# Memory attention with a sticky expert layer: the token sums of the first softmax as one product a group instead of one a head

## The chip, the cores and the metric

The kernel runs on one core of a Trainium2 chip. The time is that of the device for one launch, in microseconds (us); lower is better. The core has a matrix engine (PE; its weight loads are listed apart as PEld), a vector engine (DVE), a scalar engine (ACT), a general engine (POOL) and a queue that issues transfers (SP). They run side by side and wait for one another through semaphores.

## What is computed

For each of 8 batches and 8 heads, 576 tokens with 64 features each are squeezed into 32 memory rows, which are then attended to. The output of that goes through an expert layer whose expert "sticks" from token to token. The part that matters here is the first softmax, over the tokens (axis 2):

```python
def _attn_ref(q, k, v, phi):
    a = phi - np.max(phi, axis=2, keepdims=True)
    a = np.exp(a)
    a = a / (np.sum(a, axis=2, keepdims=True) + 1e-09)
    k_m = np.einsum('bhsm,bhsd->bhmd', a, k)
    v_m = np.einsum('bhsm,bhsd->bhmd', a, v)
    ...
    attn = softmax(scale * q @ k_m.T)          # over the 32 memory rows
    return attn @ v_m
def _moe_ref(x, w_gate, w_local, w1, w2):
    ...
    out[b, s] = p[e] * (np.maximum(x[b, s] @ w1[e], 0.0) @ w2[e])
```

The divisor `np.sum(a, axis=2)` is one number for each batch, head and memory row: 8 heads by 32 rows, 256 numbers a batch.

## The kernel before

The heads of a batch stand in two groups (`NG` = 2) of four (`HG` = 4). Head 2h + g has its 576 tokens on the 64 partitions `half[g]`: partitions 0 to 63 for group 0, 64 to 127 for group 1, nine tokens on each. A tile of 128 partitions so holds both groups at once.

For each batch the chain of the first softmax runs through these steps, each a function and a name in the list of steps:

- "phi", "kv": the transfers of phi and of k and v. "colmax" to "cx": a maximum over all tokens. "sub", "exp": subtraction and exponential, in place in `pt`.
- "asum" (L310, on DVE; in batch 0 L386 and L387, in batch 1 on POOL): adds the nine tokens of a partition, so that `asum` is 128 partitions by 4 heads by 32 memory rows.
- "pkv" (L396): the unnormalised `k_m` and `v_m`. 72 products a batch, each with weights of 64 partitions by 32 columns (one head, one of nine tokens) and 128 moving columns; the output goes to 32 partitions of the accumulator `pkv[g]`, those of head h.
- "sums" (`f_sums`, L407): adds `asum` over the 64 partitions of a group, by a product with a column of ones. Eight products a batch, each with weights of 64 partitions by 32 columns and one moving column; the output is column 128 of `pkv[g]`, partitions 32h to 32h + 31.
- "rinv" (L418, L419, on DVE): adds 1e-9 to that column and takes the reciprocal. "kvn" (L427, on ACT; one in batch 0 on DVE, L429): scales `pkv` by it. "pT" (L435), "kvT" (L440): transpose and copy. `kvT` is what the scores (`k_psc`, L507), the first expert product (`w_pg`, L787) and the gate (`f_pgg`, L453) read.

The rest of the time of PE goes to the expert layer: the hidden part "ph" (L819) and the output part "po" (L857 to L859 and, for the turned half, L907 to L909), with 128 weight columns and 256 to 512 moving columns each.

The order on every engine is written out by hand. The steps of batch 0, and the first ones of batch 1, stand in `start()`, with `warm(n)` issuing n idle products "wp" (L305) between them. After that the loop over the batches runs through the expert layer of batch b, and a table of places (`PLACES`) says how far into it each step of the later batches is put in. For "sums" the table gives one number a batch. In batches 1 to 4 the products of the sums stand between two products of the expert layer; in batch 0 and in batches 5 to 7 they come right behind those of "pkv". Neither the table nor any other order is altered.

## Time and profile before

| what | value |
|---|---|
| median of 3 runs | 415.64 us (414.85 to 418.31) |
| the profiled execution's own time | 416.56 us |
| span of its instructions | 414.8 us |
| granted TensorE clock, mean over the span | 0.999 |
| records of L407 (sums) in the trace, PE and PEld each | 128, from 14.8 to 303.5 us |

In this page each product with 32-bit weights is listed as two records, a weight load (PEld) and a matmul (PE) for each of two passes: the 8 batches with 8 products of the sums each make 64 products and 128 records. A line with "x16" is a run of 16 such records, with the start of the first and the time from there to the end of the last. "64*32" is the form in which a product takes the array: 64 rows and 32 columns.

The span is the time from the first instruction to the last; the execution's own time is 1.8 us longer.

### The profile page before, as it was taken

What the parts mean: (1) busy time and instruction counts of PE and PEld (TensorE: products, weight loads), DVE (VectorE), ACT (ScalarE), POOL (GpSimd) and SP (SyncE); (2) the same over time, 40 slices, a digit from 0 to 9 for tenths busy, and PEclk for the clock granted to TensorE, in tenths of its full rate; (3) what the DMA queues carried; (4) which work ended last, traced back from release to release, by engine and by line L of the source; (5) the groups of instructions that cost most, each with busy time, mean ns of one, the idle gap of its engine ahead of it and who ended that gap; (6) DMA issues with size and microseconds to landing.
All of it is one profiled execution on the core that took longest, in us unless ns stands there. A gap on an engine that the chain in (4) does not pass through costs nothing.

```text
span 414.8 us, 10606 instructions
## 1 busy us (share of the span) xinstructions
PE 395.0 (95%) x4195; PEld 326.7 (79%) x4195; DVE 284.4 (69%) x714; ACT 177.8 (43%) x427; POOL 150.9 (36%) x162
## 2 busy tenths in 40 slices
PE   8778898999999989999999999999999999999994
PEld 2546866798777977699778997789878996899884
DVE  4487788878976797886759767777757676625300
ACT  2154652436442744435541564336541564146010
POOL 3024541536241744038510681029410660156000
PEclk9999999999999999999999999999999999999999
DMA  8969793999197939798789198965974087202011
GB/s 238 286 224 291 167 372 122 199 283 378 31 351 127 371 131 246 174 379 299 228 162 399 37 300 152 297 244 164 241 134 170 2 246 253 82 0 65 25 40 55
DMA packets 115445, 82.58 MB, mean 199 GB/s; under 512 B 69616, under 2 KB 89088, under 8 KB 115392
## 3 DMA queue, kind: packets, MB, share of 16 engines
q1 hardware_dynamic: 115328, 81.84, 66.4%
q8 instruction: 35, 0.57, 0.6%
q14 instruction: 18, 0.15, 0.1%
q0 software_dynamic: 64, 0.02, 0.1%
HBM read 66.60 MB, written 15.24 MB: 197 GB/s over the span
## 4 chain that ended last, share of the span: by engine, by line
PE 79%; DMA 11%; DVE 5%; issue 1%; SPq 1%; ACT 1%; DVEq 0%
PE ph L819 22%; PE po L907 8%; PE po L857 8%; PE po L908 7%; PE po L909 7%; PE po L859 7%; PE po L858 7%; DMA att_d<-at 6%; DMA kv_t<-in_v_dram 5%; PE pkv L396 4%; PE pg L787 3%; PE psc L507 2%; PE pl L604 1%; DVE h L829 1%; PE po L881 1%
## 5 line engine op out<-in xcount | busy, mean ns | idle before, releaser
L777 POOL TENSOR_TENSOR w2l<-raw,w2h 128x512 fp32r<-128x512 f32 x64 | 82.0, 1303 | 31.2 <-ACT w2h L776 23.5
L819 PE MATMUL ph<-ah,Gh 128*128 128x256 f32 (+1 forms) x256 | 74.5, 306 | 1.4 <-DVE h L829 1.3
L829 DVE SCALAR_TENSOR_TENSOR h<-ph,h 128x320 fp32r<-128x320 f32 (+2 forms) x104 | 52.7, 519 | 31.9 <-ACT h L827 31.5
L819 PE MATMUL ph<-ah,Gl 128*128 128x256 f32 (+1 forms) x256 | 71.6, 295 | 0.0
L907 PE MATMUL po<-h,w2l 128*128 128x320 f32 x224 | 71.5, 319 | 0.0
L909 PE MATMUL po<-h,w2h 128*128 128x320 f32 x224 | 69.2, 309 | 0.0
L908 PE MATMUL po<-h,w2h 128*128 128x320 f32 x224 | 69.2, 309 | 0.0
L827 ACT ACTIVATE h<-ph 128x320 fp32r<-128x320 f32 (+1 forms) x96 | 46.4, 489 | 44.7 <-PE ph L819 44.4
L857 PE MATMUL po<-w2h,h 128*128 128x512 f32 (+1 forms) x152 | 60.7, 399 | 0.0
L914 POOL TENSOR_TENSOR oT<-oT,gT 128x320 f32<-128x320 f32 x28 | 20.7, 741 | 104.3 <-DVE oT L913 97.4
L859 PE MATMUL po<-w2h,h 128*128 128x512 f32 (+1 forms) x152 | 57.8, 380 | 0.0
L858 PE MATMUL po<-w2l,h 128*128 128x512 f32 (+1 forms) x152 | 57.7, 379 | 0.0
L819 PE MATMUL ph<-al,Gh 128*128 128x256 f32 (+1 forms) x256 | 54.8, 295 | 0.0
L819 PEld LDWEIGHTS ph<-ah,Gh 128*128 128x128 f32 x256 | 48.1, 188 | 7.6 <-issue 3.6
L819 PEld LDWEIGHTS ph<-ah,Gl 128*128 128x128 f32 x256 | 48.2, 188 | 0.0
L563 POOL TENSOR_TENSOR al<-at,ah 128x576 fp32r<-128x576 f32 (+1 forms) x18 | 23.1, 1289 | 64.7 <-ACT ah L559 42.8
L907 PEld LDWEIGHTS po<-h,w2l 128*128 128x128 f32 x224 | 42.0, 188 | 5.6 <-issue 5.2
L776 ACT ACTIVATE w2h<-raw 128x512 fp32r<-128x512 f32 x64 | 38.4, 625 | 11.9 <-PE po L909 10.1
L908 PEld LDWEIGHTS po<-h,w2h 128*128 128x128 f32 x224 | 42.1, 188 | 0.2
L909 PEld LDWEIGHTS po<-h,w2h 128*128 128x128 f32 x224 | 42.1, 188 | 0.0
L819 PEld LDWEIGHTS ph<-al,Gh 128*128 128x128 f32 x256 | 41.1, 188 | 0.1
L857 PEld LDWEIGHTS po<-w2h,h 128*128 128x128 f32 x152 | 28.6, 188 | 14.3 <-issue 9.4
(153 smaller groups left out, 578.6 us busy)
## 6 DMA issues: line engine op xcount, KB each, us to landing
raw<-in_moe_w_dram SPq DMA_DIRECT2D x34, 512.0 KB, 6.2
raw<-in_moe_w_dram SPq DMA_DIRECT2D x15, 1024.0 KB, 6.9
kv_t<-in_k_dram SPq DMA_DIRECT2D x7, 1152.0 KB, 8.7
kv_t<-in_v_dram SPq DMA_DIRECT2D x7, 1152.0 KB, 11.2
q_t<-in_q_dram SPq DMA_DIRECT2D x112, 72.0 KB, 3.3
att_d<-at SPq DMA_DIRECT2D x8, 576.0 KB, 9.8
out_dram<-oT SPq DMA_DIRECT2D x28, 160.0 KB, 5.6
out_dram<-ot SPq DMA_DIRECT2D x17, 256.0 KB, 6.0
```

What stands on the lines that cost most here:

```text
L563: (eng or nc.gpsimd).tensor_tensor(out=st.al[:, gs, ss], in0=st.at[:, gs, ss], in1=st.ah[:, gs, ss], op=ALU.subtract)
L776: nc.scalar.activation(h, src, AF.Copy)
L777: nc.gpsimd.tensor_tensor(out=l, in0=src, in1=h, op=ALU.subtract)
L819: nc.tensor.matmul(pv[:, c - c0], lhsT=lt[:, g, cs], rhs=rt[:, g, s0 : s0 + n], start=(i == 0), stop=(i == 5),)
L827: nc.scalar.activation(hc[:, :, 0:n], pv, AF.Relu)
L829: nc.vector.scalar_tensor_tensor(out=hc[:, :, o : o + z - a], in0=pv[:, :, a:z], scalar=0.0, in1=hc[:, :, a:z], op0=ALU.max, op1=ALU.subtract,
L857: nc.tensor.matmul(po[:, c0:c1], lhsT=h[:, c, th], rhs=hi, start=(c == 0), stop=False)
L858: nc.tensor.matmul(po[:, c0:c1], lhsT=h[:, c, th], rhs=lo, start=False, stop=False)
L859: nc.tensor.matmul(po[:, c0:c1], lhsT=h[:, c, tl], rhs=hi, start=False, stop=(c == FC - 1))
L907: nc.tensor.matmul(po[:, 0:n], lhsT=lo, rhs=h[:, c, 0:n], start=(c == 0), stop=False)
L908: nc.tensor.matmul(po[:, 0:n], lhsT=hi, rhs=h[:, c, 0:n], start=False, stop=False)
L909: nc.tensor.matmul(po[:, 0:n], lhsT=hi, rhs=h[:, c, n : 2 * n], start=False, stop=(c == FC - 1))
```

## The change

`f_sums` issues one product for each group instead of one for each group and head. Its weights are the four heads' sums side by side, 64 partitions by 128 columns, and its output is the whole column 128 of `pkv[g]`, all 128 partitions. The same numbers come out at the same places: row 32h + m of the output is the sum of head h and memory row m. The number of products falls from 64 to 16 in the whole kernel.

```diff
     def f_sums(st):
-        for h in range(HG):
-            for g in range(NG):
-                nc.tensor.matmul(
-                    st.pkv[g][32 * h : 32 * h + 32, P : P + 1],
-                    lhsT=st.asum[half[g], h],
-                    rhs=ones[half[g]],
-                    start=True,
-                    stop=True,
-                )
+        for g in range(NG):
+            nc.tensor.matmul(
+                st.pkv[g][:, P : P + 1],
+                lhsT=st.asum[half[g]].rearrange("p h m -> p (h m)"),
+                rhs=ones[half[g]],
+                start=True,
+                stop=True,
+            )
```

Each engine keeps its order. Behind the edit every line number is smaller by one, so that L407 becomes L406 and L435 becomes L434.

On PE in batch 5, where the sums stand right behind "pkv" (an output of 32 partitions by 128 columns reads 32x128), before:

```order
L396 MATMUL pkv<-kv_t,phi_t 32x128 [waits Activation_49]
L396 MATMUL pkv<-kv_t,phi_t 32x128 x23
L407 MATMUL pkv<-ones,asum 32x1 [waits DVE_49]
L407 MATMUL pkv<-ones,asum 32x1 x7
L857 MATMUL po<-w2h,h_2872 128x512
```

and after:

```order
L396 MATMUL pkv<-kv_t,phi_t 32x128 [waits Activation_49]
L396 MATMUL pkv<-kv_t,phi_t 32x128 x23
L406 MATMUL pkv<-ones,asum 128x1 [waits DVE_49]
L406 MATMUL pkv<-ones,asum 128x1
L856 MATMUL po<-w2h,h_2842 128x512
```

The two products stand where the eight stood, the first of them with the same wait for DVE, and the next neighbours are the same.

On PE in batch 4, where the sums stand between products of the expert layer, there is one more difference, some rows further on, at the transposes pT. Before:

```order
L859 MATMUL po<-w2h,h_2150 128x512
L407 MATMUL pkv<-ones,asum 32x1 [waits DVE_49]
L407 MATMUL pkv<-ones,asum 32x1 x7
L857 MATMUL po<-w2h,h_2150 128x512
...
L435 MATMUL pT<-ident,kvn 128x128 [waits Activation_49] x2
```

and after:

```order
L858 MATMUL po<-w2h,h_2126 128x512
L406 MATMUL pkv<-ones,asum 128x1 [waits DVE_49]
L406 MATMUL pkv<-ones,asum 128x1
L856 MATMUL po<-w2h,h_2126 128x512
...
L434 MATMUL pT<-ident,kvn 128x128 [waits PE_49,Activation_49]
L434 MATMUL pT<-ident,kvn 128x128 [waits Activation_49]
```

The first transpose of batch 4 now also waits for an earlier product of PE itself, the last one of the gate step L604, which stands ahead of the sums. No other wait is added or taken away on any engine.

## The prediction

> **What bounds the kernel now.** I read the page's chain of work first, since it says which engine's time counts.

> ```profile
> PE 395.0 (95%) x4195; PEld 326.7 (79%) x4195; DVE 284.4 (69%) x714; ACT 177.8 (43%) x427; POOL 150.9 (36%) x162
> PE 79%; DMA 11%; DVE 5%; issue 1%; SPq 1%; ACT 1%; DVEq 0%
> ```

> PE is busy for 95% of the span and carries 79% of the chain. A tenth of a microsecond more or less in its queue mostly reaches the end. So the question is what the sums cost PE now, and what they will cost.

> Second, the sums by their own line, with minimum, median and maximum duration.

> ```profile
> L407 PEld LDWEIGHTS pkv<-ones,asum x128: 102/106/107, 14.8 to 303.5; 64*32 64x32 f32 x128
> L407 PE MATMUL pkv<-ones,asum x128: 163/167/188, 14.9 to 303.5; 64*32 64x1 f32 x128
>   DVE rinv L418: 6.2, 3
> ```

> 128 records of some 167 ns would be 21 us one after another. They are not one after another, as the order in time shows. First batch 2, where the sums stand alone between products of form 128*128 (columns: start, duration of the run, engine):

> ```profile
> 86.17 0.31 PE L908 MATMUL po<-h,w2h 128*128 128x320 f32 x1
> 86.32 0.31 PE L909 MATMUL po<-h,w2h 128*128 128x320 f32 x1
> 86.56 0.27 PE L407 MATMUL pkv<-ones,asum 64*32 64x1 f32 x16
> 86.75 0.41 PE L907 MATMUL po<-h,w2l 128*128 128x320 f32 x1
> 87.00 0.30 PE L908 MATMUL po<-h,w2h 128*128 128x320 f32 x1
> ```

> All 16 records take 0.27 us, of which 0.167 is one record: 16 starts lie within 0.10 us. The expert products normally start 0.15 apart (86.17, 86.32). Around the sums two things are added. At each change of form the next product starts only about 0.07 before the end of the last one (86.32 + 0.31 = 86.63 against 86.56; 86.83 against 86.75), so the overlap of neighbours is lost twice. And the first product after it takes 0.41 instead of 0.31.

> Then batch 5, where the sums follow pkv in the same form 64*32, and the place of batch 2 where a product of another form follows pkv directly:

> ```profile
> 209.08 0.63 PE L396 MATMUL pkv<-kv_t,phi_t 64*32 64x128 f32 x27
> 209.45 0.29 PE L407 MATMUL pkv<-ones,asum 64*32 64x1 f32 x16
> 209.68 0.50 PE L857 MATMUL po<-w2h,h 128*128 128x512 f32 x1
> ...
> 84.94 0.61 PE L396 MATMUL pkv<-kv_t,phi_t 64*32 64x128 f32 x26
> 85.48 0.41 PE L907 MATMUL po<-h,w2l 128*128 128x320 f32 x1
> ```

> In the same form the sums start 0.26 before pkv's end (209.71 against 209.45), and they end at 209.74, only 0.03 later than pkv. Into another form the start is 0.07 before the end (85.55 against 85.48). So in batches 0, 5, 6 and 7, where the sums follow pkv, they cost almost nothing now.

> The chain of work over time has the sums in it at every batch; the first, one standing alone, and the last:

> ```profile
> 15.07 0.12 PE pkv L407 x14
> 86.63 0.20 PE pkv L407 x13
> 303.57 0.13 PE pkv L407 x15
> ```

> With four such stretches of about 0.20 and four of about 0.13, plus 0.10 for the first product behind each lone block, 4 x 0.30 + 4 x 0.13 = 1.7 us is all that any change to this step can win.

> **The change part by part.** It removes 12 of the 16 matmul records of each step, and makes the others 128 columns wide instead of 32. What does a wide one cost? No row shows 64 rows by 128 columns with one moving column, so I bound it. Weight loads by width:

> ```profile
> L578 PEld LDWEIGHTS pl<-ggt,at 128*1 128x1 f32 x32 | 1.1, 81 | 4.0 <-issue 1.9 <-DVE at L555 1.3 <-ACT qT L497 0.4
> L355 PEld LDWEIGHTS pm<-ident,mc 128*64 128x64 f32 x32 | 1.6, 134 | 2.3 <-DVE mc L350 0.6 <-issue 0.6 <-DVE l L592 0.4
> L907 PEld LDWEIGHTS po<-h,w2l 128*128 128x128 f32 x224 | 42.0, 188 | 5.6 <-issue 5.2
> ```

> 1, 32, 64 and 128 columns take 81, 105 (the sums now), 134 and 188 ns: some 80 fixed and about 0.84 ns a column, so 107 ns for 128 columns against 25 for 32. The nearest blocks of four records, each behind a change of form:

> ```profile
> 64.13 0.24 PE L578 MATMUL pl<-ggt,at 128*1 128x8 f32 x4 [1.11 <-DVE at L555]
> 22.45 0.44 PE L355 MATMUL pm<-ident,mc 128*64 128x128 f32 x4
> 24.56 0.43 PE L493 MATMUL pq<-ident,q0e 32*128 32x32 f32 x4
> L355 PE MATMUL pm<-ident,mc x32: 272/298/323, 6.8 to 287.2; 128*64 128x128 f32 x32
> L493 PE MATMUL pq<-ident,q0e x8: 221/222/243, 15.1 to 24.8; 32*128 32x32 f32 x8
> ```

> L355 is nearest in kind: two products on two separate parts of the array, two passes each. Its block of 0.44 less one record of 0.27 leaves 0.16 of starts for two passes, so the two products run side by side, and the first pass is longer by 0.05 (323 against 272), which is its load of 64 columns. For the new sums I take the same with 128 columns: the first pass 0.10 longer (as 0.41 against 0.31 at L907), the second 0.107 behind it, the other group 0.007 beside. Starts spread over 0.22 us, and with one record of 0.167 the block takes **0.39 us**. Low end: L493, 128 columns of weights but 32 rows: 0.43 less 0.222 is 0.21 for three steps, the first longer by 0.02, so two passes side by side need 0.02 + 0.063 + 0.007 = 0.09, a block of 0.26. High end: nothing side by side, 0.10 + 3 x 0.107 + 0.167 = 0.59.

> Sums standing alone (batches 1 to 4): 0.39 instead of 0.27, **+0.12 each**; both changes of form are there already. In batch 1 I cost it at nothing:

> ```profile
> 40.34 0.60 ACT L827 ACTIVATE h<-ph 128x512 fp32r<-128x512 f32 x1 [1.86 <-PE ph L819]
> 40.65 0.28 PE L819 MATMUL ph<-ah,Gl 128*128 128x256 f32 x1
> 41.02 0.39 PE L819 MATMUL ph<-ah,Gh 128*128 128x256 f32 x1
> ```

> There PE stands for 0.37 between starts that are otherwise 0.12 apart, until ACT is done at 40.94 with a tile from before the sums: 0.25 of cover for 0.12. Without this cover it would be 0.12 more. So 3 x 0.12 = 0.36.

> Sums behind pkv (batches 0, 5, 6, 7): the form now changes, 64*32 to 64*128, which the trace never shows. If it is a change like the others, the sums start 0.07 before pkv's end instead of 0.26, 0.19 later, and end 0.39 after that: 209.64 + 0.39 = 210.03 against 209.74, **+0.28 each** with the decimals kept, 1.13 in all. If the array keeps going between two forms of 64 rows, it is only the +0.12, or less. I take the change of form as drained, because every change in the rows above is, in both directions. [...] No run so far shows this pair of forms.

> Behind PE: `rinv` on DVE waits for the sums three times (6.2 us in the rows above, most of it idle time in batch 0) and will start 0.1 to 0.3 later. Queued behind it on DVE are transposes and expert evictions; ACT's `kvn` and then pT wait for it. In batch 0 all of it moves with PE, whose queue between sums and pT is filled by idle products, so nothing is added beyond the +0.28. Later pT comes microseconds after the sums. The new wait of pT in batch 4 is for a product that is some microseconds old; the price of such a wait in PE's queue is a 51 ns event, hidden behind products in flight, and 0.05 if not:

> ```profile
> L435 PEldq EVENT_SEMAPHORE  x2: 51/51/51, 16.2 to 309.0; - x2
> ```

> No transfer, SP instruction or POOL instruction is moved.

> Sum: 0.36 + 1.13 = **+1.5 us**, nearly all of it on the chain. The profiled execution took 416.56, with a span of 414.8; it would become 418.1. The median shown is 415.64, 0.9 below that execution, so I forecast **417.1 us**. A change within 1%, 4.2 us, can't be told from none by measuring this kernel; this is 0.4%.

> **The rivals.**

> *Nothing side by side.* The two groups share the 128 columns, and the four passes run one behind another: a block of 0.59, 0.20 more for seven steps, and batch 1 leaves its cover by 0.07. 1.5 + 1.5 = +3.0, 418.6 us. Against it: the eight products of L407 on eight places start 16 records in 0.10, and half of these share their columns with another.

> *The load is cheap.* Block 0.26 as at L493: the lone ones gain nothing, those behind pkv cost 0.19 - 0.03 = 0.16: +0.6, 416.2 us. For it: L493 is the only row with fewer than 128 rows and 128 columns. Against: its weights are for a transpose, and 107 ns fits all the other widths.

> *Cost goes by the number of products.* Four records at the spacing of L578, (0.24 - 0.17) / 3 = 0.025, and no drain between two forms of 64 rows: a block of 0.24, -0.03 for the three lone ones and -0.04 for the four others (0.26 early and 0.24 long, it ends before pkv, and the next starts 0.07 before pkv's end, at 209.64 instead of 209.68), -0.25 us: 415.4. Against it: the width of the load would have to cost nothing. [...]

> *A transfer slips.* The side of a clear loss. The chain has this stretch, and the page's list of transfers the median of its kind:

> ```profile
> 50.16 12.93 DMA att_d<-at
> att_d<-at SPq DMA_DIRECT2D x8, 576.0 KB, 9.8
> ```

> This store has 3.1 us above the median when others share the queues. If the delay of 0.28 in batch 0 moves another store of the eight from the median to this, off PE's cover, that is 1.5 + 3.1 = +4.6, 420.2 us. It decides from 2.7 us of slip on. Against it: SP's order stays, and all that leads to these issues moves together.

> **How the numbers follow.** Forecast 55%, cheap load 17%, nothing side by side 14%, by number of products 8%, a transfer slips 5%; 1% for a transfer that happens to come earlier by as much. The first four lie between 415.4 and 418.6. Widened by what the lowest run lies under its median (0.8) below and by half of that above, the range is 414.6 to 419.0. Faster by over 1%: 0.01. Slower by over 1%: the slipped transfer, 0.05. Within 1%: 0.94.

> **What would show it.** In the new profile L406 should have 32 records of form 64*128 with weight loads of about 188 ns, in blocks of four that take 0.39 us (0.26: cheap load; 0.59: nothing side by side; 0.24: by number). In batches 5 to 7 the block should start 0.07 before pkv's end and 0.26 before it if nothing drains. `po` behind it should still have its first record 0.1 longer. Wrong would be the forecast if the span grows or shrinks by more than these blocks do, which would put the cause in another queue.

## The result

The changed kernel took 421.94 us (median of 4 runs, 421.29 to 423.66), against 416.98 us for the one before (median of 4 runs, 414.85 to 418.31). The ratio is 1.0127 with a 95% interval of 1.0089 to 1.0164: slower by 5 us. The interval is clear of no change, and the time lies above the range of 414.6 to 419.0. Its profiled execution took 421.71 us.

The page after, in the lines that answer to those shown of before (PEclk is the clock granted to PE in 40 equal slices of the span, in tenths of full speed):

```profile
span 419.9 us, 10411 instructions
PE 398.3 (95%) x4095; PEld 328.5 (78%) x4099; DVE 285.9 (68%) x714; ACT 177.6 (42%) x427; POOL 151.2 (36%) x162
PE 83%; DMA 7%; DVE 5%; issue 2%; SPq 1%; ACT 1%; DVEq 0%
PEclk9999999999999998999999999999999999999999
```

The span is 5.1 us longer. PE has 96 to 100 records fewer and is busy for 3.3 us more. Two things in it were not forecast: "issue", time in which an engine waits for nothing that the profile shows, is 2% of the chain instead of 1%, and in the sixteenth slice the clock granted to PE is not full.

First the sums themselves. In order of time on PE, batch 2, where they stand alone, and batch 5, where they follow pkv (columns: start, duration of the run, engine):

```profile
85.97 0.31 PE L908 MATMUL po<-h,w2h 128*128 128x320 f32 x1
86.21 0.39 PE L406 MATMUL pkv<-ones,asum 64*128 64x1 f32 x4
86.53 0.42 PE L906 MATMUL po<-h,w2l 128*128 128x320 f32 x1
...
213.23 0.76 PE L396 MATMUL pkv<-kv_t,phi_t 64*32 64x128 f32 x36
213.92 0.39 PE L406 MATMUL pkv<-ones,asum 64*128 64x1 f32 x4
214.23 0.50 PE L856 MATMUL po<-w2h,h 128*128 128x512 f32 x1
```

The block takes 0.39 us in both. In batch 5 it starts at 213.92, 0.07 before pkv ends at 213.99; before the change it was 0.26. So between these two forms of 64 rows the overlap is lost, as at the other changes of form (0.07 between `po` and the sums of batch 2 as well: 86.28 against 86.21). The prediction calls this drained; the traces show when the products start, not what the array does in between.

The rest of the loss is at one place, which the sums have no part in: the 16 records of the gate products of batch 3 (L604 before, L603 after) that follow the pkv products of batch 4. PE in order of time, before:

```profile
162.69 0.74 PE L604 MATMUL pl<-at,ggt 128*32 128x160 f32 x16
163.36 0.50 PE L857 MATMUL po<-w2h,h 128*128 128x512 f32 x1
163.69 0.39 PE L858 MATMUL po<-w2l,h 128*128 128x512 f32 x1
...
164.94 0.27 PE L407 MATMUL pkv<-ones,asum 64*32 64x1 f32 x16
```

and after:

```profile
161.78 0.47 PE L603 MATMUL pl<-at,ggt 128*32 128x160 f32 x7
165.55 0.85 PE L603 MATMUL pl<-at,ggt 128*32 128x128 f32 x9 [3.30 <-issue]
166.33 0.80 PE L856 MATMUL po<-w2h,h 128*128 128x512 f32 x1
166.92 0.63 PE L857 MATMUL po<-w2l,h 128*128 128x512 f32 x1
...
169.08 0.39 PE L406 MATMUL pkv<-ones,asum 64*128 64x1 f32 x4
```

After seven of the 16 records PE stands for 3.30 us in the middle of a run of like products, with no wait in front of the eighth. Behind the hole a product of 512 columns takes 0.63 instead of 0.39. The stages around it (columns: stretch, its length, busy time of each engine, then granted clock, share of the DMA engines, GB/s):

```profile
163.00:165.00 2.00, 0.00 (x0) 0.00 (x0) 0.00 (x0) 0.00 (x0) 0.00 (x0) 1.00 0.54 62
165.00:167.00 2.00, 1.45 (x11) 0.96 (x12) 0.41 (x2) 0.13 (x1) 0.00 (x0) 0.62 0.65 106
167.00:169.00 2.00, 2.00 (x6) 1.25 (x4) 0.00 (x0) 0.82 (x4) 0.00 (x0) 0.52 0.76 123
```

For two microseconds no engine does anything; then PE runs at half clock (0.50 granted in every stretch from 165.55 to 168.50). The starts of the same step in the two traces give the account. The gate products start 0.91 us earlier after the change than before (161.78 against 162.69), `po` behind them 2.97 later (166.33 against 163.36), the sums 4.14 later (169.08 against 164.94), and the span ends 5.1 later. So the hole with its neighbourhood costs 3.9 us and the half clock behind it 1.2. The last 1.0 is a balance. The wide sums of batches 4 to 7 add 0.12 and three times 0.28. Against that, PE waits 0.52 for a tile `at` at 279.71 in the kernel before alone, which gives 0.6 back. PE's last product so ends 4.54 later (413.60 against 409.06), and the other 0.6 comes up behind it. Of the 0.91 won ahead of the hole, 0.8 is a smaller hole that only the kernel before has, in the pkv products of batch 3: they take 3.07 us before and 2.25 after, and the wide sums behind them give 0.12 of this back. The smaller hole, in the chain of before:

```profile
124.56 2.08 PE pkv L396 x130
126.64 0.47 issue
127.11 0.45 PE pkv L396 x14
```

### The profile page after: what moved, and what is told of

Read it like the earlier page. It is cut to its first block, busy times and chain, and to the rows that moved or that the text cites. A ratio compares the mean times of both kernels' runs of the same rounds, so it can differ in the third digit from the quotient of the medians.

```text
span 419.9 us, 10411 instructions
## 1 busy us (share of the span) xinstructions
PE 398.3 (95%) x4095; PEld 328.5 (78%) x4099; DVE 285.9 (68%) x714; ACT 177.6 (42%) x427; POOL 151.2 (36%) x162
## 4 chain that ended last, share of the span: by engine, by line
PE 83%; DMA 7%; DVE 5%; issue 2%; SPq 1%; ACT 1%; DVEq 0%
PE ph L818 21%; PE po L906 9%; PE po L856 8%; PE po L908 8%; PE po L907 8%; PE po L857 7%; PE po L858 7%; DMA kv_t<-in_v_dram 4%; PE pkv L396 4%; PE pg L786 3%; DMA att_d<-at 3%; PE psc L506 2%; PE pl L603 1%; DVE h L828 1%; PE po L880 1%
## 5 line engine op out<-in xcount | busy, mean ns | idle before, releaser
L908 PE MATMUL po<-h,w2h 128*128 128x320 f32 x224 | 69.2, 309 | 0.0
L907 PE MATMUL po<-h,w2h 128*128 128x320 f32 x224 | 69.2, 309 | 0.0
L857 PE MATMUL po<-w2l,h 128*128 128x512 f32 (+1 forms) x152 | 58.4, 384 | 0.4 <-POOL w2l L776 0.4
L907 PEld LDWEIGHTS po<-h,w2h 128*128 128x128 f32 x224 | 42.1, 188 | 0.2
L908 PEld LDWEIGHTS po<-h,w2h 128*128 128x128 f32 x224 | 42.1, 188 | 0.0
## 6 DMA issues: line engine op xcount, KB each, us to landing
att_d<-at SPq DMA_DIRECT2D x8, 576.0 KB, 7.6
```

Source lines behind the costliest of these rows:

```text
L857: nc.tensor.matmul(po[:, c0:c1], lhsT=h[:, c, th], rhs=lo, start=False, stop=False)
L907: nc.tensor.matmul(po[:, 0:n], lhsT=hi, rhs=h[:, c, 0:n], start=False, stop=False)
L908: nc.tensor.matmul(po[:, 0:n], lhsT=hi, rhs=h[:, c, n : 2 * n], start=False, stop=(c == FC - 1))
```

## The theories

*Program fetch.* By this theory PE reads its program in pieces. The page has a queue "q8 instruction" (columns: packets, MB, share of the DMA engines), before and after:

```profile
q8 instruction: 35, 0.57, 0.6%
...
q8 instruction: 34, 0.56, 0.6%
```

These are packets of 16 KB (0.57 MB by 35). By the theory each is a piece, and if one is used up before the next has landed, PE stands, with nothing to wait for. The traces have 8,460 records of PE's queue (products, weight loads and wait events) before and 8,265 after, some 242 and 243 a packet. The change takes 24 instructions from each batch (12 matmul records and 12 weight loads), which moves the places where the pieces end. The expectations take 256 instructions for a piece, 64 bytes each: at first an assumption, which these two pages do not show and the count further down does.

*Wide products.* The loss hangs on the new blocks and on what waits for them.

*Transfers collide.* The small shift in time makes some transfer late.

Two kinds of run tell them apart: the changed kernel with small extra products that put the program's length back, and the kernel before, its sums untouched, with extra products that move it. The expectations call the place "the gate products of batch 4"; it is the gate of batch 3 behind the pkv of batch 4, and the hole is the same. All times are medians, beside the kernel before on the same chip; the ratios and their intervals are as recorded, and are not the quotients of the two medians.

## The length put back in every batch

```diff
                         stop=(c == TN - 1),
                     )
+        if cs.stop < TN:
+            return
+        for i in range(6):
+            g, h = i % NG, i // NG
+            nc.tensor.matmul(
+                st.pkv[g][32 * h : 32 * h + 32, P + 1 : P + 2],
+                lhsT=ident[half[g], 0:32], rhs=ones[half[g]],
+                start=True, stop=True,
+            )
```

> The changed kernel, with six small extra products (64 rows, 32 columns, one moving column, the form of the batch's other products) behind the last pkv product of every batch, so that PE's program has as many matrix instructions in front of every later step as before the change. Their output goes to a column that nothing reads. Theory 'program fetch' (the 3.3 us hole in batch 4 comes from where the 16 KB pieces of PE's program end, which the 24 instructions less a batch have moved): the hole near 162 us is gone, the clock stays at full, and what is left is the direct price of the wide blocks, some +1.5 us plus 0.05 a batch for the extra products: 417 to 419 us against 416 to 417 before. Theory 'wide products' (the loss hangs on the wide blocks themselves and what waits for them): the hole stays and the time is 421 to 423 us. Theory 'transfers collide' (the shift in time by some 0.3 us a batch makes transfers late): hole stays too, since the shift in time stays.

Measured: 418.44 us against 417.05, ratio 1.0042 (1.001 to 1.0074). PE at the place of the hole:

```profile
161.09 2.25 PE L396 MATMUL pkv<-kv_t,phi_t 64*32 64x128 f32 x144
163.08 0.26 PE L408 MATMUL pkv<-ones,ident 64*32 64x1 f32 x12
163.28 0.74 PE L615 MATMUL pl<-at,ggt 128*32 128x160 f32 x16
163.94 0.50 PE L868 MATMUL po<-w2h,h 128*128 128x512 f32 x1
```

The sums are as wide as in the changed kernel, and 48 products more are issued, but the 16 gate records run through and the clock stays full. The two rivals are out: neither expected the hole to go. What is left is 1.8 us by the ratio and 1.4 by the medians, of which the extra products themselves may be up to 0.4, as was estimated ahead of the run.

## The length moved from the start

Three runs had their extra products in PE's idle time before the first pkv of batch 0: 24 in the changed kernel, 40 and 64 in the kernel before.

```diff
+    def pad_stream(n):
+        for i in range(n):
+            h = i % HG
+            nc.tensor.matmul(
+                wt[0][32 * h : 32 * h + 32, 0:1],
+                lhsT=ident[:, 0:32], rhs=ones, start=True, stop=True,
+            )
...
+        pad_stream(40)      # 24 and 64 in the other two
         for i in range(2):
             f_asum_piece(s, i)
```

> The changed kernel, with 24 small extra products (96 records) in PE's idle time before the first pkv of batch 0, so that PE's program up to batch 4 is as long as before the change. Theory 'program fetch': no hole at the gate products of batch 4, 416.5 to 419 us; holes can come up in other batches, where the count still differs. Theories 'wide products' and 'transfers collide': 421 to 423 us, as without the padding.

> The kernel before, its sums untouched, with 40 small extra products (160 records) in PE's idle time before the first pkv of batch 0. If a piece of PE's program is 16 KB and an instruction 64 bytes (256 a piece), 160 more moves the ends of the pieces at batch 4 to where 96 fewer put them. Theory 'program fetch': a hole of about 3 us near the gate products of batch 4 with a stretch of half clock behind it, although no sum was changed, 419 to 422 us. Theory 'wide products': no change, 415 to 418 us. Theory 'transfers collide': no change, since the padding hides in idle time.

> The kernel before with 64 small extra products (256 records, one whole piece of PE's program) at the same place. Control for the padding. Theory 'program fetch': the ends of the pieces fall where they fell before, no hole in batch 4, within 1 us of the kernel before (up to 1 us for the padding if the idle time does not hold it). If this one has the hole too, it is the padding that makes it and the run with 160 tells nothing. Theory 'wide products' and 'transfers collide': the same as before.

Measured: 425.54 us (ratio 1.0191, 1.015 to 1.0232), 425.95 us (1.0221, 1.0174 to 1.0268) and 423.75 us (1.0166, 1.0107 to 1.0225). By their totals all three missed what program fetch expected: the control is slow too, so the padding itself costs several microseconds at this place. The traces say why. The kernel before with 40 products has the forecast hole, although no sum was changed:

```profile
163.51 0.47 PE L616 MATMUL pl<-at,ggt 128*32 128x160 f32 x7
167.58 0.85 PE L616 MATMUL pl<-at,ggt 128*32 128x128 f32 x9 [3.60 <-issue]
```

With 64 it is not there; but the start has a new one, in the first products of batch 0:

```profile
17.02 1.27 PE L408 MATMUL pkv<-kv_t,phi_t 64*32 64x128 f32 x33 [2.59 <-issue]
```

There the next packet landed at 15.43. The changed kernel with 24 products has no hole behind the pkv of batch 4, as expected, but two others of 2.62 and 2.89 us, at 17.79 and 44.97. So the padding used up the early pieces of the program while the next was still to come, and a cleaner place was needed.

## The length moved from batch 1

In batch 1 PE stands idle for 1.4 us ahead of the gate step pgg. In the trace of before pgg starts there at 49.34 and is record 1334 of PE's queue; the packet that goes with the next end of a piece, at record 1472, had landed at 44.82. At the start, at record 448, it landed at 17.24, 0.27 before PE came to it, and PE stood until 18.54. The same products were put there, writing to a column of `pgg` that nothing reads:

```diff
         st.pgg = [ps_a.tile([P, 512], F32, tag="pa", name="pgg") for g in range(NG)]
+        for i in range(40 if st.b == 1 else 0):      # 64, 24, 12
+            h = i % HG
+            nc.tensor.matmul(
+                st.pgg[0][32 * h : 32 * h + 32, 256:257],
+                lhsT=ident[:, 0:32], rhs=ones, start=True, stop=True,
+            )
```

> The kernel before, its sums untouched, with 40 small extra products (160 records, some 0.85 us) at the gate step pgg of batch 1, where PE stands idle for 1.4 us. Unlike at the start, PE's program runs well ahead there. Theory 'program fetch': holes at records 448 + 256 k alone; the one at record 4032, in the gate products of batch 4, of 3 to 4 us, followed by 3.4 us at half clock, and holes of about 0.5 us in batches 6 and 7, so +4 to +6 us: 421 to 423 us where before has 417. Theory 'wide products': no hole, within 1 us of before. Theory 'transfers collide': no hole, since nothing behind batch 1 moves in time.

> The control: 64 small extra products (256 records, some 1.25 us, one whole 16 KB piece) at the same place. Theory 'program fetch': behind batch 1 the ends of the pieces fall where they fell before; no hole in batch 4 and full clock there, so within 1 us of before; a hole of up to 1 us in batch 1 itself, where the padding uses a piece up quickly, is possible. Theories 'wide products' and 'transfers collide': the same as before. Whoever holds that padding as such costs some 4 us expects it here as in the run with 160.

> The changed kernel with 24 small extra products (96 records) at the same place, which puts the ends of the pieces in batch 4 back to where they were before. Theory 'program fetch': no hole at the gate products of batch 4, 417.5 to 419 us, which is before and the direct price of the wide blocks of about 1.5. Theories 'wide products' and 'transfers collide': 421 to 423 us.

> The kernel before with 12 small extra products (48 records) at the same place: a try at a version better than both. Theory 'program fetch': the end of a piece that now lies 20 records inside the pkv block of batch 3 moves to 28 records ahead of it, so the hole of 0.5 to 0.7 us at record 3008 of the kernel before goes, and none comes up in the other batches: 0.5 us less than before, ratio 0.998 to 1.000. Theories 'wide products' and 'transfers collide': the same as before, and the hole in batch 3 stays.

| kernel | extra records | median us | ratio to before (95%) | hole behind the pkv of batch 4 |
|---|---|---|---|---|
| before | 160 | 422.60 | 1.0147 (1.0089 to 1.0205) | 3.92 us |
| before | 256 | 416.26 | 1.0006 (0.9979 to 1.0033) | none |
| changed | 96 | 417.42 | 1.0001 (0.9972 to 1.003) | none |
| before | 48 | 417.67 | 1.0021 (0.9992 to 1.005) | none |

The kernel before had 416.9 us in these. With 160 records, PE at the place, in a kernel with the old sums:

```profile
163.64 0.47 PE L613 MATMUL pl<-at,ggt 128*32 128x160 f32 x7
168.02 0.85 PE L613 MATMUL pl<-at,ggt 128*32 128x128 f32 x9 [3.92 <-issue]
168.80 0.80 PE L866 MATMUL po<-w2h,h 128*128 128x512 f32 x1
```

Of the two holes of about 0.5 us that were expected in batches 6 and 7, only that of batch 7 is there (0.45). With 256, the changed kernel with 96, and the kernel before with 48 (there the place of its own small hole, the pkv of batch 3):

```profile
162.45 0.74 PE L613 MATMUL pl<-at,ggt 128*32 128x160 f32 x16
...
163.56 0.74 PE L612 MATMUL pl<-at,ggt 128*32 128x160 f32 x16
...
124.67 2.25 PE L396 MATMUL pkv<-kv_t,phi_t 64*32 64x128 f32 x144
```

More padding costs less: 160 records make the old kernel some 6 us slower, 256 leave it as it was. That is what pieces of 256 instructions foretell and nothing else in question. The last run was the try at a better kernel. It took the small hole of batch 3 away, as expected, but the gain of 0.5 us did not show: 1.0021, not told from 1.

All records of PE's queue are counted from the start of the trace: products, weight loads and the queue's own wait events. Then every hole of PE of more than 0.4 us that no wait explains, in all runs of this study (the last is told of below), lies within three records of 448 + 256 k:

```
kernel                     holes at record          448 + 256 k
before                     449, 3010                448, 3008
changed                    448, 3774                448, 3776
changed, same count        1214                     1216
changed, 96 at start       448, 1214, 2237          448, 1216, 2240
before, 160 at start       448, 4030, 6077, 7101    448, 4032, 6080, 7104
before, 256 at start       450, 1470                448, 1472
before, 160 in batch 1     4034, 7105               4032, 7104
before, 256 in batch 1     3266                     3264
changed, 96 in batch 1     none
before, 48 in batch 1      none
changed, half of w1        450, 3778                448, 3776
```

## Why the piece comes late

In the changed kernel PE enters the piece that ends in the hole at 159.9 us, 0.3 us into a dense stretch: pkv with 288 records and the gate with 32 would pass in under 3 us. So nearly the whole piece is dense, and PE is through it at 162.25, in 2.4 us. In the kernel before a piece ends in the middle of this stretch, at 161.89, but that piece and the next one reach into the slower expert products on either side and last 6.9 and 9.3 us. The packet with the next piece starts at 162.74 by the trace's record of packets, lands at 164.27, and PE goes on at 165.55, 1.28 later. All 19 holes of the list end so, between 1.28 and 1.63 us after a packet of q8 has landed. Meanwhile the DMA engines are taken up by the two transfers of w1 for batch 3, 2 MB issued at 154.57:

```profile
157.00:160.00 3.00, 3.00 (x43) 2.27 (x43) 2.65 (x5) 1.55 (x3) 2.15 (x2) 1.00 1.04 399
160.00:162.00 2.00, 2.00 (x143) 1.73 (x119) 2.00 (x2) 1.26 (x2) 0.63 (x1) 1.00 1.10 363
```

To see whether the packet waits behind them, batch 3 loads half of w1 and uses it twice; the other half is left out, so the output of batch 3 is another:

```diff
+            hs = slice(0, 2) if st.b == 3 else slice(0, HG)
-            nc.sync.dma_start(out=raw[:, :, n * j : n * j + n], in_=w1v[:, :, f0 : f0 + n])
+            nc.sync.dma_start(out=raw[:, hs, n * j : n * j + n], in_=w1v[:, hs, f0 : f0 + n])
...
-                    rhs=st.raw1[n][half[g], h, part],
+                    rhs=st.raw1[n][half[g], h % 2 if st.b == 3 else h, part],
```

> The changed kernel, but batch 3 loads only the first two of the four row blocks of w1 and uses them twice: its two w1 transfers are 512 KB instead of 1024 KB each, so the output of batch 3 is another. PE's program is the same, instruction for instruction. In the changed kernel PE enters the last piece before the hole at 159.9 us, but the next 16 KB packet starts at 162.7 only, when the two w1 transfers issued at 154.6 are nearly through (163.1). Theory 'the packet waits behind the weight transfers': with half of the bytes they are through by about 160, the packet starts 2 us or more earlier and the hole of 3.3 us shrinks to less than 1.2 us, the half clock behind it goes, and the time is 416.5 to 418.5 us. Theory 'a packet takes that long anyway': the hole stays at 3 us or more and the time at 421 to 423 us.

Measured: 418.06 us against 417.10, ratio 1.002 (0.9988 to 1.0052). The profiled execution took 423.16, and at 152.83, ahead of this place, PE is already 5.4 us behind where the changed kernel's trace has it; so only this place is read from it:

```profile
167.19 0.47 PE L603 MATMUL pl<-at,ggt 128*32 128x160 f32 x7
168.78 0.52 PE L603 MATMUL pl<-at,ggt 128*32 128x128 f32 x9 [1.13 <-issue]
169.23 0.50 PE L857 MATMUL po<-w2h,h 128*128 128x512 f32 x1
```

The program is the same, and PE stops at the same record; but the packet starts 0.87 us after PE enters the piece before it, instead of 2.87, the hole is 1.13 us, and `po` behind it takes 0.50 instead of 0.80: no half clock. So with half of the transfers the packet starts 2.0 us sooner and the hole is 2.2 us shorter. The parts add up: with all of w1, 2.87 until the packet starts, 1.53 until it lands and 1.28 until PE goes on, less the 2.38 that the piece itself lasts, are 3.30; with half, 0.87, 1.33 and 1.31 less 2.39 are 1.12. The transfers were not through as early as expected: the second landed 6.9 us after the issue of the first, against 8.5 with all of w1. The other profiles point the same way: in all eleven, the packet that falls into these two transfers starts between 0.8 us before and 0.04 us after the second of them has landed, while PE had entered its piece 0.9 to 3.2 us earlier. So at this place the packet waits for these transfers, and the hole is as long as that wait makes it. Full DMA engines alone did not hold every packet up as long: in the kernel before, one started 1.5 us after PE entered its piece at 138.62, with 398 GB/s in flight. Whether it is the bytes on one of the 16 DMA engines or the number of packets that counts was not tried.

## The prediction, point by point

**What PE pays for the old sums.** Held as far as it went: a block of 0.27, and 0.03 behind pkv. The limit of 1.7 us on what a change to this step can win was drawn from PE's own records alone, and so was every loss.

**The block of 0.39.** It came out at 0.39, but from other parts, so that the total agrees is luck. The starts spread over 0.14 us, not 0.22, and one record lasts 0.25, not 0.167:

```profile
L406 PEld LDWEIGHTS pkv<-ones,asum x32: 182/184/187, 14.9 to 307.9; 64*128 64x128 f32 x32
L406 PE MATMUL pkv<-ones,asum x32: 246/258/268, 14.9 to 308.0; 64*128 64x1 f32 x32
```

The weight load of 184 ns is close to the 188 of the estimate by width. The record is 0.08 us longer than an old one, about what the wider load adds, and the spacing is shorter than forecast; that the load's time sits in the record's length is not shown further. The two groups run side by side, so "nothing side by side" is out, and with 0.39 so are "the load is cheap" and "by the number of products".

**The change of form.** Held: +0.12 where the sums stand alone, +0.28 behind pkv.

**The direct sum of +1.5 us.** In the three kernels with wide sums and without the long hole the ratio is 1.0042, 1.0001 and 1.002: 1.8, 0.0 and 0.8 us, each uncertain by about 1.3. Their mean of 0.9 does not tell 1.5 from half of it. Part of it may be won back: the changed kernel with 96 records has none of the holes that the kernel before has. In the trace of the changed kernel PE falls back by 0.12 at the sums of batches 2, 3 and 4 and by 0.28 at those of 5, 6 and 7, 1.2 us together. The 0.28 of batch 0 can't be read off: behind it PE waits for transfers of w1, until 33.44 before and 33.38 after, and these waits take it up.

**The rival "a transfer slips".** Its size, +4.6, was near the measured loss, by luck; it was given 5%, and it named the wrong transfer: a store of `at` that PE waits for. The late transfer was one of PE's own program.

**The step that failed** is the first sentence of the part on the change: that it "removes 12 of the 16 matmul records of each step, and makes the others 128 columns wide". It was costed as time on the array only. What it also does is to shorten PE's program by 24 instructions a batch, 96 by batch 4, and so to move the pieces of 16 KB until one of them lay nearly whole within a dense stretch. PE was through it in 2.4 us, the next piece was not there for another 3.30, and the half clock behind that cost 1.2 more. "No transfer ... is moved" left out the queue that carries the program. The signs stood in the trace of before: two stretches named "issue", 0.84 us at 17.70 and 0.47 at 126.64, in the middle of runs of like products, and the queue q8 on the page. The prediction read past both. With the count of records they could have told that such holes come up, and where; the size of 3.3 us, which hangs on the weight transfers ahead of the packet, could not have been read from them.

## What to carry to other kernels

Count a change in the number of small products twice: once on the array, and once as a shift of the program. A hole in the middle of a run of like products with nothing that ends it was, wherever it fell on this count, a program that was not there yet: all 19 ended 1.28 to 1.63 us after a packet of q8 had landed. Count the records up to it, and see whether the holes of two kernels lie a multiple of one piece apart, which was 256 records here. Before such a change is judged, run it once with the instruction count put back: here it was 1.3% slower as written, and within 0.5% of before with the count restored.

## What was not expected of the hardware

- PE used up a piece of 256 instructions in 2.4 us where products are as small as pkv's (159.87 to 162.25), while the next packet, in the changed kernel with all and with half of w1, took 2.9 and 0.9 us to start, 1.5 and 1.3 us to land, and another 1.3 us until PE went on.
- A hole of 3.3 us was followed by about 3.4 us at half clock (0.50 granted from 165.55 to 168.50; 0.62 and 0.52 in the stages shown, the first with the end of the hole in it), which cost another 1.2 us; holes of 0.47 and 1.13 us were not.
- In the kernel before, the pkv products of batches 5, 6 and 7 begin at records 4609, 5628 and 6648 of the count: some 1020 records a batch, four less than four pieces, so that the pieces end at nearly the same step of each of these batches. In the changed kernel they begin at 4486, 5481 and 6477, some 996 a batch, and the ends wander by 28 records from batch to batch.
